# Loads of v and z moved to SyncE's queue with casts on the engines, later places for work that waits for transfers, and one more block of scores turned

## The chip, the cores and the metric

The kernel runs on one core of one Trainium2 chip. The metric is the time of one execution in microseconds (us) on the device; several runs are taken and their median stands for the kernel. The core has a matrix engine (TensorE, PE in the profile, with PEld for its weight loads), VectorE (DVE), ScalarE (ACT), GpSimd (POOL) and SyncE (SP), which here only issues transfers. Each engine works through its own list of instructions in order and waits on semaphores for the others. Transfers are issued from an engine's queue and run on 16 DMA engines.

## The reference

Two stages follow each other, for 8 batches of 3,200 rows:

```python
# stage 1: gated attention, u and v (8, 3200, 256), z (8, 3200, 64)
scores = (1 / S) * z @ z.T                 # S = 3200, symmetric
x = u * (np.maximum(scores, 0) ** 2 @ v)
# stage 2: token mixing, w_q and w_k (256, 64), w_out (256, 256)
wq, wk = x @ w_q, x @ w_k
mixed = (1 / 8) * (wq @ wk.T) @ x          # computed as wq @ (wk.T @ x)
out = np.maximum(mixed, 0) @ w_out
```

All inputs and the output are fp32. The kernel multiplies in fp16 and accumulates in fp32.

## The kernel before

**Tiles and stages.** A batch's 3,200 rows are 25 tiles of 128, in seven groups: six of 512 columns (four tiles) and a last one of 128. For a group `gi` and a row tile `ti`, `scores` (L263) multiplies a tile of z by the group's columns. Two such tiles make a pair, in one PSUM slot of 128 x 1,024; there are two slots, shared with the other small products. `first_stage` (L286 on ScalarE, L290 on VectorE) evicts the pair through a relu into `g`, `second_stage` (L306 on ScalarE, L308 on GpSimd) squares it into `at` in fp16 (16 buffers). `second_product` (L351) multiplies `at` by v into accumulators, in two halves of a group; `gate` (L368, L369, L388) sums the two accumulators of a half and multiplies by u into `x_sb`.

**Turned blocks.** The scores are symmetric, so the block of groups (gi, gj) is also the transpose of the block (gj, gi). `is_turned` says which blocks are computed once and transposed by a DMA (`turn` in `second_stage`, L330, into `tt` or `ttl`): those with `gj` at most two groups behind `gi` (`FAR = 2`), and all that end in the last group. `SKIP` takes one out in batch 0; `EXTRA`, empty before, adds blocks in the other batches. The others are computed twice.

**Stage two.** `turn_x` (L400) transposes x by a DMA, `projections` (L417) makes queries and keys, `turn_keys` (L436) transposes the keys, `double` (L448) doubles them, `heads` (L455) sums keys times x, `mix` (L483) and `proj` (L521) make the output, which `proj_out` (L546, L551) scales and SyncE stores (L552).

**Loads.** In batch 0, z and v come in pieces (L110, L113). For the next batches `load_v` (L150, five pieces of five tiles) and `load_z` (L156, one piece) are issued from GpSimd's queue, and the transfer itself changes fp32 to fp16. `turn_z` (L163) transposes z by four DMAs on SyncE's queue. u is loaded on SyncE's queue (L174).

**The order.** Nothing schedules at run time. While the program is built, a planner in the kernel keeps a clock for each engine (`clock`, `give`), takes one step of TensorE after another, and so writes out the order of every engine's instructions. Its main loop takes a waiting extra step (keys, heads, mix, proj), a pair (`use_pair`) or an accumulation step (`acc_step`); pairs run ahead of the accumulation by `lead` steps. Transfers of SyncE wait in `moves` with a ready time and a due time; `flush` sends the one that is due first once the planned queue is free, and `send` adds the planned time of issue (`issue`) and of the DMA engines (`takes`), with a backlog of `RING`, and says when it lands (`LANDS` later). What needs a transfer is given a place after that time: x after `XWAIT`, a turned block's rows 0.5 us after landing, keys at landing. `squares` chooses ScalarE or GpSimd with `SPARE`, `choose` ScalarE or VectorE with `BIAS`.

Of the kernel before, what the change touches and what calls it, by code (L numbers as in the profile page):

```python
# [16 lines left out]
def kernel(  # L17
# [48 lines left out]
    pg = ctx.enter_context(tc.tile_pool(name="pg", bufs=7))  # L66
# [80 lines left out]
    def load_v(b, n0, nn):  # L147
        if n0 == 0:
            vs[b] = pv.tile([P, NT, D], FP16, tag="v_sb", name="v_sb")
        nc.gpsimd.dma_start(out=vs[b][:, n0 : n0 + nn, :], in_=rows(v, b)[:, n0 : n0 + nn, :])  # L150
# [3 lines left out]

    def load_z(b):
        nc.gpsimd.dma_start(out=zn[:, 1 : NT + 1, :], in_=rows(z, b))  # L156
# [54 lines left out]
    EXTRA = []  # L211
# [388 lines left out]
    MIXES = 10.0  # L600
# [9 lines left out]
    RING = 2.0  # L610
# [47 lines left out]
    UNTIL = 24.0  # L658
# [36 lines left out]
    def squares():  # L695
        while pending and pending[0][0] <= clock[PE] + 0.3:
# [9 lines left out]
            for (b, gi, gj, _, nn, _, _), turn in second_stage(p, g, ways):  # L706
# [4 lines left out]
                    done + SLACK, due + SLACK, 1.28, 0.21 * n, turn,  # L711
# [20 lines left out]
    def use_keys(b, gi):  # L732
# [17 lines left out]
        if not final:  # L750
            move(
                done + SLACK, done + 10.0, 1.28, 0.21 * n, lambda: turn_keys(b, gi),
                lambda t: at_time(t, lambda: double(b, gi)),
# [63 lines left out]
    def project_out(b, gi, ps, ready):  # L817
# [14 lines left out]
        move(done + SLACK, done + 6.0, 0.55, 1.6, stores[0], landed)  # L832

    def push(takes):
        give(POOL, clock[PE], 0.6)
        dma_at[0] = max(dma_at[0], clock[PE]) + takes

    Z0 = 24
    ZWAIT, ZDUE, ZSTEP, ZSTEP0 = 14.0, 32.0, 7.0, 5.0
    V0 = 56  # L840
    V1 = 10

    def batch_begun(b, t):
        if b + 1 < B:
            t0 = max(t + 6, Z0)
            at_time(t0, lambda: (load_z(b + 1), push(3.0)))
            step = ZSTEP if b else ZSTEP0
            for i, (_, m0, m1) in enumerate(ZTURNS):
                move(
                    t0 + ZWAIT + step * i, t0 + ZDUE + step * i, 1.28, 0.21 * (m1 - m0),  # L850
                    lambda i=i: turn_z(b + 1, i),
                    lambda t, i=i: z_ready.update({(b + 1, i): t}),
                )
            for i in range(5):
                at = t + 20 + 13 * i if b else V0 + V1 * i
                at_time(at, lambda i=i: v_loaded(b + 1, 5 * i, 5))

    def v_loaded(b, n0, nn):
        load_v(b, n0, nn)
        push(2.5)  # L860
        for n in range(n0, n0 + nn):
            v_at[b, n] = dma_at[0] + 5.0
# [7 lines left out]
    def group_begun(b, gi, t):  # L870
        if gi == 0:
            batch_begun(b, t)
        if gi + 1 < NG:
            move(max(t + 2, clock[POOL] + SLACK), t + 7, 0.55, 1.6, lambda: load_u(b, gi + 1))
        elif b + 1 < B:
            move(max(t + 2, clock[POOL] + SLACK), t + 7, 0.55, 1.6, lambda: load_u(b + 1, 0))

    SPARE = 0.5
    BIAS = 0.2
    XDUE = 5.0  # L880
    XWAIT = 2.0
    LATE = 0.5

    def half_done(b, gi, half):
# [10 lines left out]
        if half == halves(gi)[-1]:  # L895
            n = 8 if widths[gi] == W else 2
            move(
                t + SLACK, t + XDUE, 1.28, 0.21 * n, lambda: turn_x(b, gi),
# [122 lines left out]
    move(10.0, 14.0, 0.55, 1.6, lambda: load_u(0, 0))  # L1021
# [5 lines left out]
    lead = 140  # L1027
    turn_about = False
    while groups or work or current["left"]:
# [10 lines left out]
                and (x[1] != "proj" or all(t + 2.0 <= now for t in stored[-2:]))  # L1040
# [134 lines left out]
```

## Time and profile before

| | us |
|---|---|
| median of 3 runs | 775.03 |
| lowest, highest | 774.68, 778.61 |
| the profiled execution | 773.15 |
| its span, first to last instruction | 770.9 |
| mean granted TensorE clock | 0.997 |

The page of the profile shows each engine's busy time as a share of the span, 28,221 instructions in all. A group's line names the kernel's line, the engine, the operation, what it writes and reads, the count, then busy time and mean of one in nanoseconds, and the idle time of the engine just before with what ended it. The windows give busy time per engine in a stretch of the span. The chain of waits follows the work that ended last back from the last instruction. For transfers, a view gives the time from issue to landing. Busy TensorE time is modelled from pipelined products; two products of 64 rows each run side by side, so their durations overlap.

### The profile page before, as it was taken

How to read it: one execution, taken by the hardware profiler on the slowest of the kernel's cores; microseconds unless marked ns; L12 is line 12 of the kernel's file. 1: busy time of each engine (PE TensorE's matmuls, PEld its weight loads, DVE VectorE, ACT ScalarE, POOL GpSimd, SP SyncE). 2: the span in 40 equal slices, each digit the busy share in tenths (PEclk: the TensorE clock that was granted, in tenths of full speed). 3: DMA queues.
4: the chain of work that ended last, by engine and by line, in shares of the span. 5: the costliest groups of instructions: out<-in, count | busy, mean ns of one | idle time of the engine just before them, and what ended most of it. 6: DMA issues, size and time to landing. Idle time of an engine off the chain costs nothing.

```text
span 770.9 us, 28221 instructions
## 1 busy us (share of the span) xinstructions
PE 761.7 (99%) x12408; PEld 678.4 (88%) x12408; DVE 510.5 (66%) x537; ACT 561.2 (73%) x647; POOL 591.1 (77%) x496
## 2 busy tenths in 40 slices
PE   8999999999999999999999999999999999999996
PEld 7889998888898888989889988998889989898884
DVE  6775876675787566765677756765667476675645
ACT  7785876778758678875788677877777676777734
POOL 8796788789687778666778687887878887888740
PEclk9999999999999999999999999999999999999998
DMA  8999999999999999999899999999999998979625
GB/s 199 130 187 182 167 204 173 160 212 194 194 162 189 194 209 190 182 213 203 153 190 162 188 231 163 219 145 160 262 156 192 184 190 211 201 143 203 152 84 191
DMA packets 307114, 141.09 MB, mean 183 GB/s; under 512 B 285744, under 2 KB 288432, under 8 KB 306992
## 3 DMA queue, kind: packets, MB, share of 16 engines
q1 hardware_dynamic: 300224, 123.13, 85.0%
q0 software_dynamic: 6624, 15.98, 14.8%
q8 instruction: 97, 1.59, 0.9%
q14 instruction: 25, 0.20, 0.1%
q10 hardware_dynamic: 144, 0.20, 0.1%
HBM read 59.64 MB, written 26.21 MB: 111 GB/s over the span
## 4 chain that ended last, share of the span: by engine, by line
PE 94%; POOL 2%; DVE 1%; DMA 1%; ACT 1%; issue 1%; POOLq 0%; SPq 0%; DVEq 0%; ACTq 0%
PE acc L351 68%; PE sc L263 13%; PE fo L521 6%; PE qk L417 3%; PE qk L455 2%; POOL at L308 2%; PE mx L483 1%; DMA z<-in_z_dram 1%; POOL x_sb L388 1%; DVE g L290 0%; ACT g L286 0%; DVE fo L546 0%; DMA xT_sb<-x_sb 0%; PE hd L455 0%; ACT at L306 0%
## 5 line engine op out<-in xcount | busy, mean ns | idle before, releaser
L351 PE MATMUL acc<-v_sb,at 64*128 64x256 f16 x7344 | 504.7, 269 | 0.0
L308 POOL TENSOR_TENSOR at<-g 128x1024 f16<-128x1024 f32 (+1 forms) x218 | 402.3, 1859 | 71.6 <-ACT g L286 29.1
L351 PEld LDWEIGHTS <-at 64*128 64x128 f16 x7344 | 407.2, 94 | 48.1 <-issue 4.8
L290 DVE TENSOR_SCALAR g<-sc 128x1024 f32<-128x1024 f32 (+2 forms) x285 | 338.5, 1203 | 122.8 <-PE sc L263 114.3
L306 ACT ACTIVATE at<-g 128x1024 f16<-128x1024 f32 (+2 forms) x255 | 257.2, 1023 | 21.8 <-DVE g L290 17.8
L286 ACT ACTIVATE g<-sc 128x1024 f32<-128x1024 f32 (+2 forms) x186 | 183.2, 989 | 76.8 <-PE sc L263 75.0
L388 POOL TENSOR_TENSOR x_sb<-both,u_sb 128x512 f16<-128x512 f32 (+1 forms) x112 | 135.8, 1217 | 81.6 <-DVE both L369 77.7
L263 PE MATMUL sc<-zT 64*128 64x512 f16 x924 | 188.1, 375 | 1.4 <-DVE g L290 0.6
L351 PE MATMUL acc<-v_sb,tt 64*128 64x256 f16 x2272 | 163.4, 269 | 0.0
L351 PEld LDWEIGHTS <-tt 64*128 64x128 f16 x2272 | 126.2, 94 | 10.3
L369 DVE TENSOR_TENSOR both<-acc,both 128x512 f32<-128x512 f32 (+1 forms) x104 | 69.6, 670 | 21.4 <-ACT both L368 17.0
L263 PEld LDWEIGHTS <-zT 64*128 64x128 f16 x924 | 61.2, 94 | 7.6 <-issue 3.9
L368 ACT COPY both<-acc 128x512 f32<-128x512 f32 (+1 forms) x69 | 39.0, 565 | 38.7 <-PE acc L351 36.1
L546 DVE TENSOR_SCALAR fo<-fo 128x1024 f32<-128x1024 f32 (+1 forms) x28 | 32.4, 1166 | 46.6 <-PE fo L521 46.6
L509 ACT ACTIVATE rt<-mx 128x1024 f16<-128x1024 f32 x39 | 39.9, 1024 | 12.6 <-PE mx L483 12.1
L521 PE MATMUL fo<-wo,rt 128*128 128x256 f16 x386 | 46.6, 273 | 0.5 <-ACT rt L505 0.5
L521 PEld LDWEIGHTS <-rt 128*128 128x128 f16 x386 | 36.2, 98 | 8.4 <-issue 3.6
L431 ACT CAST qk<-qk 128x512 f16<-128x512 f32 (+1 forms) x47 | 25.3, 539 | 24.6 <-PE qk L455 20.0
L368 DVE COPY both<-acc 128x512 f32<-128x512 f32 (+1 forms) x35 | 23.6, 674 | 21.2 <-PE acc L351 19.9
L470 DVE TENSOR_TENSOR ha<-qk,ha 128x512 f32<-128x512 f32 x37 | 25.5, 689 | 14.4 <-ACT qk L431 14.1
L551 ACT ACTIVATE fo<-fo 128x1024 f32<-128x1024 f32 (+2 forms) x23 | 22.5, 978 | 16.5 <-PE fo L521 15.8
L417 PE MATMUL qk<-xT_sb,wqk 64*128 64x256 f16 (+1 forms) x404 | 32.3, 265 | 0.0
(55 smaller groups left out, 282.9 us busy)
## 6 DMA issues: line engine op xcount, KB each, us to landing
u_sb<-in_u_dram SPq DMA_DIRECT2D x48, 512.0 KB, 4.8
out_dram<-fo SPq DMA_DIRECT2D x46, 512.0 KB, 5.1
v_sb<-in_v_dram POOLq DMA_DIRECT2D x35, 320.0 KB, 6.0
zn<-in_z_dram POOLq DMA_DIRECT2D x7, 400.0 KB, 7.8
tt<-at SPq DMA_TRANSPOSE x143, 4.7
u_sb<-in_u_dram SPq DMA_DIRECT2D x8, 128.0 KB, 2.9
out_dram<-fo SPq DMA_DIRECT2D x4, 256.0 KB, 3.3
xT_sb<-x_sb SPq DMA_TRANSPOSE x56, 5.4
```

Of the source, the lines that this page charges most:

```text
L263: nc.tensor.matmul(out=sc[h][:, 0:gw] if banks else sc[:, h, 0:gw], lhsT=z_cols(b, h, ti * P, P), rhs=z_cols(b, h, gs, gw), start=True, st ...
L286: nc.scalar.activation(out=g[:, hs, 0:w], in_=part, func=RELU, scale=GSCALE)
L290: nc.vector.tensor_scalar(out=g[:, hs, 0:w], in0=part, scalar1=0.0, scalar2=GSCALE, op0=AOP.max, op1=AOP.mult,)
L306: nc.scalar.square(out=out, in_=g[:, hs, 0:w])
L308: nc.gpsimd.tensor_mul(out=out, in0=g[:, hs, 0:w], in1=g[:, hs, 0:w])
L351: nc.tensor.matmul(out=accs[half, r][:, ds((j % 2) * D, D)], lhsT=weights(b, gi, ti, j)[top(r), :], rhs=vs[b][top(r), ti, :], start=(first ...
L368: copy(out=both[:, 0 : n * D], in_=accs[half, 0][:, 0 : n * D])
L369: nc.vector.tensor_add(out=both[:, 0 : n * D], in0=accs[half, 1][:, 0 : n * D], in1=both[:, 0 : n * D])
L388: nc.gpsimd.tensor_mul(out=xs[b, gi][:, 0:n, :, r, :].rearrange("p n c d -> p (n c) d"), in0=both[:, 0 : n * D].rearrange("p (m d) -> p m ...
L417: nc.tensor.matmul(out=ps[:, r, 0 : n * P], lhsT=wqk[top(r), c, :, :].rearrange("p t h -> p (t h)"), rhs=xTs[b, gi][top(r), 0:n, c, :], st ...
L509: nc.scalar.activation(out=out, in_=part, func=RELU)
L521: nc.tensor.matmul(out=banks[r][:, ds(j * D, D)], lhsT=flat[:, ds((dc * n + j) * P, P)], rhs=wo[:, dc, :], start=(dc == 0 and j == 0), sto ...
```

## The change

v and z of the next batch are loaded by SyncE's queue as fp32, in ten parts (`PARTS`: one of z, nine of v) and then cast to fp16 by ScalarE or GpSimd (`cast_part`). Most parts land in a piece of the next batch's v tile that has not been filled yet, the others in two staging tiles (`pst`); a part that uses a place again is sent once the casts that empty it are planned to be done. For room, the `g` tiles go from 7 buffers to 6. z is sent from 6 us after a batch's beginning, and the planner places a part's cast 6 us after its planned landing.

`EXTRA` gets the block of groups 0 and 3, so in batches 1 to 7 it is computed once and turned.

The planner's figures change: more time between a landing and what needs it (`XWAIT` 2 to 9, keys 4, turned rows 3.5, stores 4 against 2), other costs of a transfer, a backlog of 1.5, `MIXES` 10 to 8, `lead` 140 to 180, `SPARE` 0.5 to 0.1, `BIAS` 0.2 to −0.2, `UNTIL` 24 to 16. `UNTIL` is the time up to which a pair's squares may be split between two engines.

```diff
-    pg = ctx.enter_context(tc.tile_pool(name="pg", bufs=7))
+    pst = ctx.enter_context(tc.tile_pool(name="pst", bufs=1))
+    pg = ctx.enter_context(tc.tile_pool(name="pg", bufs=6))
...
-    def load_v(b, n0, nn):
-        if n0 == 0:
+    STAGES = (3, 2)
+    PARTS = [
+        (False, 0, 25, 12.5, 0),
+        (True, 0, 3, 6, 0),
+        (True, 3, 5, 15, 1),
+        (True, 8, 2, 11, 2),
+        (True, 10, 3, None, 0),
+        (True, 13, 2, None, 0),
+        (True, 15, 2, 21, 3),
+        (True, 17, 3, None, 5),
+        (True, 20, 2, None, 6),
+        (True, 22, 3, None, 8),
+    ]
+    stage_of = {}
+
+    def load_part(b, i):
+        is_v, n0, nn, slot, _ = PARTS[i]
+        if i == 0:
             vs[b] = pv.tile([P, NT, D], FP16, tag="v_sb", name="v_sb")
-        nc.gpsimd.dma_start(out=vs[b][:, n0 : n0 + nn, :], in_=rows(v, b)[:, n0 : n0 + nn, :])
+        size, what = (D, v) if is_v else (dqk, z)
+        if slot is None:
+            k = STAGES.index(nn)
+            stage = pst.tile([P, nn * D], FP32, tag=f"st{k}", name="st")[:]
+        else:
+            at = int(slot * D)
+            stage = vs[b][:].rearrange("p n d -> p (n d)")[:, at : at + 2 * nn * size].bitcast(FP32)
+        stage_of[b, i] = stage.rearrange("p (n d) -> p n d", d=size)
+        nc.sync.dma_start(out=stage_of[b, i], in_=rows(what, b)[:, n0 : n0 + nn, :])
+
+    def cast_part(b, i, m0, m1, by_act):
+        is_v, n0, _, _, _ = PARTS[i]
+        copy = nc.scalar.copy if by_act else nc.gpsimd.tensor_copy
+        out = vs[b][:, n0 + m0 : n0 + m1, :] if is_v else zn[:, 1 + m0 : 1 + m1, :]
+        copy(out=out, in_=stage_of[b, i][:, m0:m1, :])
...
-    def load_z(b):
-        nc.gpsimd.dma_start(out=zn[:, 1 : NT + 1, :], in_=rows(z, b))
...
-    EXTRA = []
+    EXTRA = [(0, 3)]
...
-    MIXES = 10.0
+    MIXES = 8.0
...
-    RING = 2.0
+    RING = 1.5
...
-        dma_at[0] = max(dma_at[0], begun) + takes
         sp_at[0] = max(begun + issue, dma_at[0] - RING)
+        dma_at[0] = max(dma_at[0], begun + max(issue, 0.9)) + takes
         if landed:
-            landed(max(sp_at[0], dma_at[0]) + LANDS)
+            landed(dma_at[0] + LANDS)
...
-    UNTIL = 24.0
+    UNTIL = 16.0
...
-                row_at[b, gj, starts[gi] // P + n] = t + 0.5
+                row_at[b, gj, starts[gi] // P + n] = t + TURNS
...
-                lambda t: at_time(t, lambda: double(b, gi)),
+                lambda t: at_time(t + KEYS, lambda: double(b, gi)),
...
+    Z1 = 6
+    VTIMES = [0, 4, 18, 23, 28, 34, 40, 46, 53, 60]
+    V0 = 0.75
+    CASTS = 6.0
+    KEYS = 4.0
+    TURNS = 3.5
+    STORES = 4.0
...
     def batch_begun(b, t):
...
+        if b == 0:
+            nc.gpsimd.memset(zn[:, 0 : NT + 2 : NT + 1, :], 0.0)
+        t0 = max(t + Z1, Z0)
+        sent[b + 1], cast[b + 1] = 0, [0, 0.0]
+        for i, (is_v, _, nn, _, after) in enumerate(PARTS):
+            at = t0 + VTIMES[i] * (1.0 if b else V0)
+            move(
+                at, at + 8.0, 0.45, 0.2 + 1.5 * nn * (D if is_v else dqk) / 1024,
+                lambda i=i: part_sent(b + 1, i),
+                lambda t, i=i: at_time(t + CASTS, lambda: part_landed(b + 1, i)),
+                lambda i=i, after=after: sent[b + 1] == i and cast[b + 1][0] >= after
+                and (not after or cast[b + 1][1] + SLACK <= clock[PE]),
+            )
...
+    def part_landed(b, i):
...
+        size, most = (D, 3) if is_v else (dqk, 9)
+        for m0 in range(0, nn, most):
+            m1 = min(nn, m0 + most)
+            n = (m1 - m0) * size
+            a, c = (max(clock[x], clock[PE]) for x in (ACT, POOL))
+            t_act, t_pool = 0.19 + 0.00084 * n, 0.15 + 0.0009 * n
+            by_act = a + SPARE < c and (a + t_act <= shut() + LATE or a + 2.5 < c)
+            cast_part(b, i, m0, m1, by_act)
...
-    SPARE = 0.5
-    BIAS = 0.2
+    SPARE = 0.1
+    BIAS = -0.2
     XDUE = 5.0
-    XWAIT = 2.0
+    XWAIT = 9.0
...
-    lead = 140
+    lead = 180
...
-                and (x[1] != "proj" or all(t + 2.0 <= now for t in stored[-2:]))
+                and (x[1] != "proj" or all(t + STORES <= now for t in stored[-2:]))
```

More of the change, by code (lines that the diff above doesn't have):

```diff
@@ L830, in landed @@
                 stored[i] = t
[L832 to L836, printed above, removed]
+        move(done + SLACK, done + 6.0, 0.45, 1.7, stores[0], landed)
     Z0 = 24
-    ZWAIT, ZDUE, ZSTEP, ZSTEP0 = 14.0, 32.0, 7.0, 5.0
-    V0 = 56
-    V1 = 10
-    def batch_begun(b, t):
[L844 to L848, printed above, removed]
+    Z1 = 6
@@ L873, in group_begun @@
         if gi + 1 < NG:
-            move(max(t + 2, clock[POOL] + SLACK), t + 7, 0.55, 1.6, lambda: load_u(b, gi + 1))
+            move(max(t + 2, clock[POOL] + SLACK), t + 7, 0.45, 1.7, lambda: load_u(b, gi + 1))
         elif b + 1 < B:
-            move(max(t + 2, clock[POOL] + SLACK), t + 7, 0.55, 1.6, lambda: load_u(b + 1, 0))
-    SPARE = 0.5
-    BIAS = 0.2
+            move(max(t + 2, clock[POOL] + SLACK), t + 7, 0.45, 1.7, lambda: load_u(b + 1, 0))
+    SPARE = 0.1
+    BIAS = -0.2
     XDUE = 5.0
-    XWAIT = 2.0
+    XWAIT = 9.0
     LATE = 0.5
```

38 lines of the change are left out of this document (23 added, 15 removed).

## The prediction

> **What bounds the kernel now.** I read the page's engine line first, then TensorE's waits, the windows, the chain of waits and the groups by form. The page opens with:
>
> ```profile
> PE 761.7 (99%) x12408; PEld 678.4 (88%) x12408; DVE 510.5 (66%) x537; ACT 561.2 (73%) x647; POOL 591.1 (77%) x496
> q1 hardware_dynamic: 300224, 123.13, 85.0%
> q0 software_dynamic: 6624, 15.98, 14.8%
> ```
>
> All that TensorE waited for, longest first:
>
> ```profile
> PE warm L144 <- DVE wo L996: 1.0, 1, 1.0
> PE sc L263 <- DVE g L290: 0.6, 2, 0.4
> PE fo L521 <- ACT rt L505: 0.5, 1, 0.5
> PE ztp L130 <- POOL zd L124: 0.4, 1, 0.4
> PE sc L263 <- ACT g L286: 0.3, 1, 0.3
> PE qq L417 <- DMA xT_sb<-x_sb: 0.2, 1, 0.2
> ```
>
> The windows (PE, weight load, DVE, ACT, POOL busy; clock; DMA share; GB/s):
>
> ```profile
> 0.00:20.00 20.00, 18.05 (x232) 14.52 (x234) 13.46 (x17) 14.29 (x18) 16.59 (x21) 1.00 0.80 194
> 20.00:40.00 20.00, 19.84 (x331) 17.73 (x329) 14.71 (x16) 14.57 (x18) 15.61 (x11) 1.00 0.95 142
> 40.00:60.00 20.00, 19.42 (x314) 16.90 (x310) 15.29 (x15) 16.62 (x18) 18.85 (x18) 1.00 1.19 178
> 100.00:720.00 620.00, 619.89 (x10221) 555.17 (x10219) 412.54 (x427) 462.52 (x525) 492.66 (x406) 1.00 1.04 188
> 720.00:771.00 51.00, 44.54 (x642) 35.83 (x637) 26.59 (x34) 24.34 (x39) 18.85 (x17) 0.96 0.47 146
> ```
>
> From 100 to 720 us TensorE is busy for 619.89 of 620 us at the full clock, while the other three stand idle for 127 to 207 us. So between the ends only a change in TensorE's work can gain, and others can only lose, by making it wait. What it waited for a transfer in the whole run is 0.2 us. The idle time sits at the ends: 20.00 − 18.05, 0.16 and 0.58 us in the first 60 us (2.7 together), and the last 20 us.
>
> **The change, part by part.** *Fewer score pairs.* One block of 4 x 4 tiles per batch is turned instead of computed a second time, in seven batches: 4 tiles each, 28 score products, 14 pairs. In the changed order of instructions TensorE has 888 score products of 512 columns in place of 916; the products into the accumulators stay 10,000 (7,120 + 2,496 + 384; 224 of them read a turned block instead of a computed one). The price of a pair, from the chain and from two pieces of the timeline:
>
> ```profile
> by line: PE acc L351 68.3%; PE sc L263 12.7%; PE fo L521 5.8%; PE qk L417 2.8%; PE qk L455 2.4%; POOL at L308 1.6%; PE mx L483 1.4%; DMA z<-in_z_dram 0.6%; POOL x_sb L388 0.5%; issue 0.5%; DVE g L290 0.5%; ACT g L286 0.4%; DVE fo L546 0.3%;
> 30.46 4.37 PE acc L351 x80
> 734.85 0.38 PE L263 MATMUL sc<-zT 64*128 64x512 f16 x2
> ```
>
> 12.7% of 770.9 us over the 462 pairs of before is 0.212 us; 80 products of 256 columns in 4.37 us are 0.109 per two, so 0.219 for two of 512. At most a pair is its whole 0.38 us, the tail included in which the next products already run. 14 pairs: 3.0 us (0.212), up to 5.3 (0.38). I take 3.0: the chain counts what nothing overlaps, and the second way agrees.
>
> *Evictions and squares.* Each pair less frees about 1.0 or 1.2 us on ScalarE or VectorE and 1.06 or 1.9 on ScalarE or GpSimd. *Casts.* v and z now land as fp32 and are cast by engines: per batch five parts of 768 and five of 512 columns of v and 1,600 columns of z in three, over seven batches 91 casts, 64 on ScalarE and 27 on GpSimd. Durations:
>
> ```profile
> L290 DVE TENSOR_SCALAR g<-sc 128x1024 f32<-128x1024 f32 x278 | 335.2, 1221 | 121.8 <-PE sc L263 113.3 <-POOL at L308 3.3 <-ACT g L286 1.8
> L286 ACT ACTIVATE g<-sc 128x1024 f32<-128x1024 f32 x175 | 178.8, 1023 | 75.0 <-PE sc L263 73.2 <-POOL kx L448 0.9 <-POOL hs L477 0.6
> L306 ACT ACTIVATE at<-g 128x1024 f16<-128x1024 f32 x240 | 250.8, 1056 | 21.8 <-DVE g L290 17.8
> L308 POOL TENSOR_TENSOR at<-g 128x1024 f16<-128x1024 f32 x211 | 396.5, 1893 | 70.0 <-ACT g L286 29.1 <-DVE g L290 29.0 <-issue 9.6
> L124 ACT CAST zd<-z 128x512 f16<-128x512 f32 x1 | 0.6, 619 | 1.8 <-DMA z<-in_z_dram 1.8
> L124 ACT CAST zd<-z 128x256 f16<-128x256 f32 x1 | 0.4, 404 | 1.2 <-DMA z<-in_z_dram 1.2
> L124 POOL CAST zd<-z 128x512 f16<-128x512 f32 x1 | 0.6, 609 | 0.9 <-DMA z<-in_z_dram 0.9
> L124 POOL CAST zd<-z 128x384 f16<-128x384 f32 x1 | 0.5, 503 | 1.4 <-DMA z<-in_z_dram 1.4
> L150 POOL DMA_DIRECT2D v_sb<-in_v_dram x35 | 20.7, 591 | 0.0
> ```
>
> By the slopes (0.84 and 0.83 ns a column) 768 columns take 0.83 and 0.82 us. ScalarE: 25 x 0.62 + 27 x 0.83 + 12 of z, some 46 us; GpSimd: 10 x 0.61 + 8 x 0.82 + 9 of z, some 18. GpSimd is rid of 42 issues at 0.591 us (25 us, not in its busy time). With the evictions that move between the engines in the new order I get ScalarE about 606 us (79%), GpSimd 625 (81%), VectorE 465 (60%). All stay under TensorE, so on average the casts cost nothing. Their cover is the distance by which score pairs run ahead: counting TensorE's work in the order, half of the pairs stood at least 8.3 us ahead of their first use before and stand 12.5 ahead after (the larger lead of 180 steps against 140); the shortest beyond the first 20 us was 3.8 and is 4.9. A cast of 0.83 us, or one that waits 3 us for its data, is inside that; a wait of 5 us at the shortest place isn't, and all that is queued behind the cast on ScalarE (an eviction of scores, for which TensorE's slot waits) is late by the rest.
>
> The tightest stage is 20 to 60 us: 95.6 of 120 us are busy on the three engines. By 55 us of TensorE's work the new order has 1.5 pairs more and nine casts more (about 4 + 6 us), so the reserve shrinks from 24 to 14 us. I take nothing for it; between −1 and +2 us.
>
> *Loads on SyncE's queue, and the turns.*
>
> ```profile
> L330 SPq DMA_TRANSPOSE tt<-at x143: 1231/1354/5576, 17.1 to 713.4; - x143
> L174 SPq DMA_DIRECT2D u_sb<-in_u_dram x56: 327/529/1814, 5.0 to 738.3; - x56
> u_sb<-in_u_dram SPq DMA_DIRECT2D x48, 512.0 KB, 4.8
> u_sb<-in_u_dram SPq DMA_DIRECT2D x8, 128.0 KB, 2.9
> v_sb<-in_v_dram POOLq DMA_DIRECT2D x35, 320.0 KB, 6.0
> ```
>
> SyncE issues 77 loads more (70 of v, 7 of z) and 14 turns more: 77 x 0.53 + 14 x 1.35 = 60 us on a queue that takes its instructions in order. Past them go the turns of blocks, x, keys and z and the stores. What a late turn meets: by the order, a turned block is first used 28 us of TensorE's work or more after its last scores (26 before, leaving out the first two blocks), transposed x 20 us or more outside the last batch, transposed z 14 us or more (25 in all but the first). The last part of v is cast 4 to 10 us ahead of its batch's first product, in the first of these batches 1.3 us behind it; that part holds the last three of 25 tiles. The later places (x 9 us after its landing against 2, keys 4, turned blocks 3.5, stores 4) give each transfer 2 to 7 us more room and add no product. A load that lands 3 us late is covered; I take 0, with 0 to 7 us open (one us per batch).
>
> *One buffer fewer for the score evictions* (6 against 7), and zn's zeroing on GpSimd: VectorE waited 3.3 us for squares in all of before, behind TensorE's cover; 0.
>
> *The end.* One output projection now stands behind the last accumulation: 16 products. What they cost, from the chain, and the chain and products behind the last accumulation of before:
>
> ```profile
> 145.23 1.85 PE fo L521 x16
> 747.81 1.74 POOL x_sb L388
> 749.57 1.77 POOL x_sb L388
> 751.34 1.47 issue
> 754.52 2.34 DMA xT_sb<-x_sb
> 756.10 0.61 PE L483 MATMUL mx<-qk,hs 64*128 64x256 f16 x8 [0.17 <-DVE hs L1126]
> 756.90 0.39 PE L417 MATMUL qq<-xT_sb,wqk 64*128 64x128 f16 x4 [0.19 <-DMA xT_sb<-x_sb]
> ```
>
> The last accumulation now ends 1.85 us earlier. Behind it, the transfer landed at 756.86 us (754.52 + 2.34), when mx had been running for 0.76 us; with 1.85 us of other products ahead of it, mx takes over as the late one. What was gained ahead is given back: 0, at best −0.2.
>
> **Sum.** −3.0 us. The profiled execution took 773.15 us (770.9 and 2.25 around the span), 1.9 under the median of the three runs shown; its 770.1 corresponds to 775.03 − 3.0 = 772.0 us. About 0.5%, 3.9 us, is what a measurement of this kernel can tell from no change: under 771.15 is faster, over 778.9 slower.
>
> **The rivals.**
>
> *More than the pairs goes.* If the earlier lead also removes the waits of the first 60 us (2.7 us idle there, 1.0 of it the wait for the first memset), or a pair is worth nearer 0.38 us, the gain is 4 to 5.3 us: 769.7 to 771.0, say 770.5. For it: the limit is TensorE, and the waits on score evictions all lie in the stages that the new constants touch. Against: that stage gets more work, not less. Chance 0.32.
>
> How long v's loads of before took to land, all 35 of them:
>
> ```profile
> DMA to landing us min/median/max: 4.5/6.0/9.0
> ```
>
> *The one queue falls behind (slower).* v and z had a queue of their own; now 77 loads and all turns follow one another. For it: the two queues' packet times add up to 99.8% of the span, and the DMA share is 1.04; if none of that is slack, 14 turns of 256 KB more (3.67 MB at 85.0% of 770.9 us for 123.13 MB, 5.3 us a MB) cost 19.5 us, 791. Against: those times overlap, and TensorE waited 0.2 us for transfers. It decides once the last parts of v land later than their 4 to 10 us of cover: then each of seven batches begins late, at 1 to 3 us each (9.0 us at most against 6.0 in the middle is the spread of v's landings) 7 to 21 us, less 3.0: 779 to 793, say 782. The Trainium skill, DMA: Bandwidth & Descriptors, section SWDGE vs HWDGE vs iDMA, says that the two kinds feed different queues inside a DMA engine, which serves them in turn; by it a turn used to share with a load and now stands behind it. No row here shows the second case. By the rows of u, 384 KB more land 1.9 us later, so a turn behind the 800 KB of z would land some 4 us later, inside its 28. Chance 0.14.
>
> *The pairs go and the time stays.* The 3.0 us come back as short waits of TensorE on evictions between 20 and 60 us and at the batch starts: 774 to 775.5. It needs the 14 us of reserve to lie in the wrong places. Chance 0.06.
>
> **How the numbers follow.** The forecast as it stands has 0.48: 772.0, its own range 770.8 to 774. With the third case, "within 0.5%" has 0.54, faster 0.32, slower 0.14. From 769.5, the bottom of the first rival, to 779.0, where the slower case begins, leaves out about 0.04 below and 0.13 above.
>
> **What would show it.** After: 888 products of 512 columns on the score line, TensorE still over 99% busy from 100 to 720 us, its last accumulation some 5 us earlier (3.0 and 1.85), ScalarE and GpSimd near 79 and 81%, casts of 0.8 us with hardly any idle time before them, and no wait of TensorE for a transfer over 1 us. Wrong would be: TensorE's idle time in the middle in whole microseconds at the seven batch starts, ended by a cast or a DMA (the slower case); or a first window as full as the others (the faster one).

## The result and the profile after

The changed kernel takes 783.8 us (median of 6 runs, 782.69 to 789.5) against 775.06 for the kernel before in the same call (6 runs, 774.53 to 778.61): 1.0115 times, 95% interval 1.008 to 1.0149. It is slower by some 9 us, where 772.0 was forecast. The ratios here and below leave out runs over 1.5% longer than the fastest of their kernel, which in e1 are seven of ten, so that its median and its ratio tell different things. The profiled execution took 783.7 us, its span is 781.9.

The page of the changed kernel opens so (engines, queues, chain by engine; the chain of before by engine stands behind it for comparison):

```profile
PE 761.8 (97%) x12380; PEld 676.5 (87%) x12380; DVE 468.8 (60%) x505; ACT 593.9 (76%) x702; POOL 599.3 (77%) x495
q1 hardware_dynamic: 325088, 155.47, 99.7%
q0 software_dynamic: 576, 1.64, 1.1%
PE 83%; DMA 7%; ACT 3%; POOL 2%; issue 2%; SPq 1%; DVE 1%; ACTq 0%; DVEq 0%; POOLq 0%
```

```profile
PE 94%; POOL 2%; DVE 1%; DMA 1%; ACT 1%; issue 1%; POOLq 0%; SPq 0%; DVEq 0%; ACTq 0%
```

TensorE has 28 products fewer (12,380 against 12,408), and no other engine came near TensorE's load. But the chain now runs through transfers for 7% of the span instead of 1%, and the packets of q1 alone fill 99.7% of the 16 DMA engines' span. The windows say where TensorE stands idle (columns as in the prediction):

```profile
0.00:20.00 20.00, 16.86 (x208) 12.93 (x209) 11.85 (x15) 14.49 (x19) 15.45 (x22) 1.00 0.74 183
20.00:40.00 20.00, 19.70 (x325) 17.52 (x323) 14.40 (x14) 16.31 (x19) 18.17 (x11) 1.00 0.92 188
40.00:60.00 20.00, 20.00 (x340) 19.19 (x337) 15.20 (x15) 17.53 (x21) 18.52 (x16) 1.00 0.95 211
100.00:720.00 620.00, 611.37 (x10048) 543.52 (x10043) 371.31 (x398) 483.26 (x562) 487.32 (x395) 1.00 1.08 210
140.00:180.00 40.00, 38.49 (x611) 34.64 (x607) 24.23 (x26) 29.99 (x37) 26.37 (x23) 1.00 1.12 202
340.00:380.00 40.00, 36.39 (x556) 31.31 (x553) 19.18 (x22) 27.48 (x35) 23.53 (x21) 0.96 1.16 226
420.00:460.00 40.00, 38.58 (x639) 34.01 (x635) 23.31 (x25) 30.69 (x37) 31.09 (x26) 1.00 1.03 196
720.00:782.00 62.00, 53.85 (x797) 44.55 (x792) 29.96 (x38) 28.54 (x43) 23.25 (x23) 0.97 0.51 154
```

The idle time of TensorE grows from 9.2 us (770.9 − 761.7) to 20.1 (781.9 − 761.8). From 100 to 720 us it is 8.63 us, where it was 0.11; in the first 60 us 3.44 against 2.69; in the last window 8.05 (the span ends at 781.9) against 6.36 (it ended at 770.9). That is the span's loss of 11.0 us but for 0.1: busy time rose by 0.1 although, by the forecast's price, 3.0 us of work went. Some 1.5 us of that is the clock of 0.96 in the 36.39 busy us of 340 to 380; where the rest went no view shows.

What TensorE waited for, and then what the other engines waited for from a transfer:

```profile
PE sc L291 <- ACT g L314: 5.0, 6, 3.4
PE ztp L131 <- POOL zd L125: 1.2, 1, 1.2
PE mx L511 <- ACT rt L537: 1.1, 1, 1.1
PE qk L445 <- ACT rtl L537: 1.0, 1, 1.0
PE sc L291 <- ACT fo L579: 0.9, 1, 0.9
```

```profile
POOL kx L476 <- DMA kx<-qk: 19.2, 7, 4.5
ACT v_sb L181 <- DMA st<-in_v_dram: 7.6, 6, 1.8
ACT v_sb L181 <- DMA v_sb<-in_v_dram: 5.4, 2, 3.8
POOL v_sb L181 <- DMA v_sb<-in_v_dram: 3.9, 1, 3.9
ACT fo L579 <- DMA out_dram<-fo: 2.2, 2, 1.2
```

TensorE still waits for no transfer. It waits for ScalarE, above all for score evictions; and ScalarE and GpSimd now wait for transfers, 38.3 us in these rows. In the kernel before, beside the first loads of z, the rows of that kind hold 4.3 us:

```profile
POOL kx L448 <- DMA kx<-qk: 2.2, 2, 2.0
POOL x_sb L388 <- DMA xT_sb<-x_sb: 1.3, 1, 1.3
ACT fo L551 <- DMA u_sb<-in_u_dram: 0.8, 1, 0.8
```

The longest stop shows how one passes to the other. SyncE's queue from 344 us on, then the chain, ScalarE and TensorE (timelines: start, duration, instruction, idle time before it and what ended it):

```profile
344.81 2.61 SPq L358 DMA_TRANSPOSE tt<-at  x2
347.46 2.38 SPq L191 DMA_TRANSPOSE zT<-zn  x1
349.94 0.53 SPq L202 DMA_DIRECT2D u_sb<-in_u_dram  x1
350.52 1.23 SPq L428 DMA_TRANSPOSE xT_sb<-x_sb  x1
351.81 0.57 SPq L175 DMA_DIRECT2D v_sb<-in_v_dram  x1
```

```profile
351.81 4.34 DMA v_sb<-in_v_dram
```

```profile
356.17 0.62 ACT L181 CAST v_sb<-v_sb 128x512 f16<-128x512 f32 x1 [3.79 <-DMA v_sb<-in_v_dram]
356.69 1.02 ACT L314 ACTIVATE g<-sc 128x1024 f32<-128x1024 f32 x1
```

```profile
353.56 0.82 PE L379 MATMUL acc<-v_sb,at 64*128 64x256 f16 x11
357.76 0.41 PE L291 MATMUL sc<-zT 64*128 64x512 f16 x2 [3.38 <-ACT g L314]
```

SyncE has three turns (two of scores, one of z), a load of u and a turn of x without a gap ahead of a part of v. The part is issued at 351.81 and lands in 4.34 us, which is not long. But ScalarE has come to its cast and waits 3.79 us; behind the cast stands the eviction of a pair of scores; and TensorE, in order too, stops for 3.38 us at the next pair, which needs the slot that this eviction frees. The same pattern (a part of v, its cast, an eviction or a copy, TensorE) ends idle times of TensorE near 157 and 460 us (0.93 and 0.48 us); at 343.8 us GpSimd had waited 3.98 us for keys, and TensorE 0.22 us behind it.

### The profile page after: what moved, and what is told of

It reads as the page before. It is cut to its first block, busy times and chain, and to the rows that moved or that the text cites. A ratio compares the mean times of both kernels' runs of the same rounds, so it can differ in the third digit from the quotient of the medians.

```text
span 781.9 us, 28324 instructions
## 1 busy us (share of the span) xinstructions
PE 761.8 (97%) x12380; PEld 676.5 (87%) x12380; DVE 468.8 (60%) x505; ACT 593.9 (76%) x702; POOL 599.3 (77%) x495
## 3 DMA queue, kind: packets, MB, share of 16 engines
q1 hardware_dynamic: 325088, 155.47, 99.7%
## 4 chain that ended last, share of the span: by engine, by line
PE 83%; DMA 7%; ACT 3%; POOL 2%; issue 2%; SPq 1%; DVE 1%; ACTq 0%; DVEq 0%; POOLq 0%
PE acc L379 60%; PE sc L291 12%; PE fo L549 4%; DMA st<-in_v_dram 3%; PE qk L445 2%; PE qk L483 2%; DMA out_dram<-fo 2%; POOL at L336 1%; DMA v_sb<-in_v_dram 1%; PE mx L511 1%; ACT g L314 1%; DMA z<-in_z_dram 1%; ACT at L334 1%; DVE g L318 1%; ACT fo L579 1%
## 5 line engine op out<-in xcount | busy, mean ns | idle before, releaser
L379 PE MATMUL acc<-v_sb,at 64*128 64x256 f16 x7120 | 486.1, 270 | 0.5 <-POOL at L336 0.3
L336 POOL TENSOR_TENSOR at<-g 128x1024 f16<-128x1024 f32 (+2 forms) x231 | 417.7, 1821 | 80.6 <-DVE g L318 71.5
L379 PEld LDWEIGHTS <-at 64*128 64x128 f16 x7120 | 392.7, 94 | 49.0 <-issue 4.7
L318 DVE TENSOR_SCALAR g<-sc 128x1024 f32<-128x1024 f32 (+2 forms) x249 | 297.0, 1202 | 170.0 <-PE sc L291 153.8
L314 ACT ACTIVATE g<-sc 128x1024 f32<-128x1024 f32 (+2 forms) x208 | 204.8, 992 | 59.7 <-PE sc L291 56.9
L334 ACT ACTIVATE at<-g 128x1024 f16<-128x1024 f32 (+2 forms) x228 | 231.3, 1039 | 8.2 <-DVE g L318 6.2
L379 PEld LDWEIGHTS <-tt 64*128 64x128 f16 x2496 | 145.0, 94 | 10.1 <-issue 0.2
L579 ACT ACTIVATE fo<-fo 128x1024 f32<-128x1024 f32 (+2 forms) x43 | 40.9, 996 | 20.3 <-PE fo L549 18.1
L476 POOL COPY kx<-kx 128x128 f16<-128x128 f16 (+1 forms) x99 | 25.6, 288 | 19.2 <-DMA kx<-qk 19.2
L539 DVE TENSOR_SCALAR rt<-mx 128x1024 f16<-128x1024 f32 x17 | 20.8, 1225 | 26.6 <-PE mx L511 26.6
```

The source lines that it names most:

```text
L314: nc.scalar.activation(out=g[:, hs, 0:w], in_=part, func=RELU, scale=GSCALE)
L318: nc.vector.tensor_scalar(out=g[:, hs, 0:w], in0=part, scalar1=0.0, scalar2=GSCALE, op0=AOP.max, op1=AOP.mult,)
L334: nc.scalar.square(out=out, in_=g[:, hs, 0:w])
L336: nc.gpsimd.tensor_mul(out=out, in0=g[:, hs, 0:w], in1=g[:, hs, 0:w])
L379: nc.tensor.matmul(out=accs[half, r][:, ds((j % 2) * D, D)], lhsT=weights(b, gi, ti, j)[top(r), :], rhs=vs[b][top(r), ti, :], start=(first ...
L579: nc.scalar.mul(out=flat_out[:, sl], in_=part, mul=FINAL_SCALE)
```

## The experiments

The table has all of them, with the kernel before of the same call.

| run | what it is | us, median (range) | before, same call | ratio (95%) |
|---|---|---|---|---|
| e1_no_loads | after, v and z loaded as before | 785.8 (773.29–800.94) | 775.99 | 1.0019 (0.997–1.0068) |
| e2_no_block | after without the block | 780.32 (776.53–782.53) | 775.99 | 1.0042 (1.0014–1.0071) |
| e3_gpsimd_queue | after, the fp32 loads from GpSimd's queue | 790.7 (784.12–798.09) | 775.99 | 1.0165 (1.0081–1.0248) |
| e4_casts12 | after, casts placed 6 us later | 807.75 (806.48–811.15) | 775.99 | 1.0416 (1.0376–1.0455) |
| e5_places_only | before with the new figures only | 777.95 (776.42–779.67) | 773.99 | 1.0056 (1.0035–1.0076) |
| e6_before_new_costs | before with the new transfer costs only | 788.32 (785.05–797.99) | 773.99 | 1.0175 (1.0148–1.0202) |
| e7_old_costs | after with the old transfer costs | 780.86 (779.77–782.55) | 773.99 | 1.0094 (1.0076–1.0113) |
| e8_block_costs15 | before, the block, a turn at 0.2 + 0.15 n | 780.26 (774.31–783.76) | 773.99 | 1.01 (1.0073–1.0127) |
| e9_light_stores | after, stores cut to a quarter | 773.7 (770.71–778.67) | 775.93 | 0.9968 (0.9942–0.9995) |
| e10_light_stores_new_costs | e6 with the same cut | 789.36 (787.19–800.53) | 775.93 | 1.0169 (1.0139–1.0198) |
| e11_block_only | before and the block, nothing else | 792.11 (790.64–797.88) | 775.93 | 1.0219 (1.0172–1.0266) |
| e12_block_mid | e8 with half the new distances | 775.02 (773.54–782.26) | 775.93 | 1.0 (0.9975–1.0026) |
| e13_before_light_stores | before with the cut of e9 | 773.96 (772.02–780.35) | 775.77 | 0.9994 (0.9965–1.0023) |
| e14_turn_cost15 | after, a turn at 0.2 + 0.15 n | 776.72 (773.13–785.18) | 775.77 | 1.0015 (0.9981–1.0048) |
| e15_turn_cost16 | after, 0.2 + 0.16 n | 783.53 (775.55–785.16) | 775.0 | 1.0082 (1.005–1.0115) |
| e16_turn_cost17 | after, 0.2 + 0.17 n | 782.32 (777.69–790.51) | 775.0 | 1.0081 (1.0047–1.0114) |

One more reading is used below. The planner writes an order, and for each transfer a time at which it is to be issued. Set against the trace, with TensorE's own drift from the plan at that moment taken off, that tells how far SyncE trails the plan. It is worked out from all of SyncE's transfers and the starts of all accumulation products of each profiled execution; the column after it is the sum of the durations of those transfers on SyncE's queue:

| run | SyncE behind its plan, us: median / 90% / most | SyncE issuing, us | last accumulation planned / run |
|---|---|---|---|
| before | −1.4 / 1.1 / 4.1 | 612 | 756.2 / 751.4 |
| after | 3.9 / 10.1 / 14.2 | 667 | 749.3 / 759.1 |
| e2_no_block | 0.5 / 6.9 / 13.6 | 627 | 755.0 / 758.4 |
| e5_places_only | 2.0 / 8.1 / 12.9 | 628 | 753.1 / 757.0 |
| e7_old_costs | −0.6 / 4.1 / 6.3 | 654 | 765.4 / 759.2 |
| e9_light_stores | 1.9 / 9.8 / 15.5 | 645 | 749.3 / 757.2 |
| e14_turn_cost15 | 5.6 / 9.6 / 12.2 | 670 | 750.4 / 753.5 |
| e16_turn_cost17 | 1.6 / 3.9 / 5.7 | 671 | 763.6 / 754.5 |

The kernel before has an order in which SyncE is ahead of its plan and TensorE beats it by 5 us. The changed kernel's order is shorter by 7 us on paper, and TensorE comes out 10 us behind it. How far SyncE trails does not rank the times, though: e14 trails as far as the changed kernel and is level with before, e16 trails far less and is 0.8% slower.

**Which part costs: e1, e2, e5, e11.** e1 takes away the loads and keeps the rest:

```diff
-        nc.sync.dma_start(out=stage_of[b, i], in_=rows(what, b)[:, n0 : n0 + nn, :])
+        nc.gpsimd.dma_start(out=vs[b][:, n0 : n0 + nn, :], in_=rows(v, b)[:, n0 : n0 + nn, :])
(and load_z, the seven g buffers and the load times of before)
```

> The block and the later places stay; v and z are loaded as before, by GpSimd's queue with the cast in the transfer. Theory A (transfers on SyncE's queue come late, casts and key copies wait for them in order on ScalarE and GpSimd, and TensorE waits for the evictions behind them): 771 to 773 us, the 3.0 us of the 14 pairs, and waits of ScalarE and GpSimd for transfers as small as before (under 5 us together). Theory B (the casts' own work fills ScalarE and GpSimd): the same 771 to 773 us. Theory C (the turned block, or the order that the new places make): 780 to 785 us.

It scattered over 28 us, too much for its time to decide anything. Its profile, of a run of 785.5 us where the ratio rests on three of 773 to 784, is only an indication: without a cast of the next batches' v and z, or a load of them on SyncE's queue, the waits for transfers were there all the same.

```profile
POOL kx L448 <- DMA kx<-qk: 24.3, 10, 5.9
ACT at L306 <- DMA ttl<-at: 9.3, 1, 9.3
PE sc L263 <- ACT g L286: 7.0, 1, 7.0
```

e2 is one line of the changed kernel:

```diff
-    EXTRA = [(0, 3)]
+    EXTRA = []
```

> Loads on SyncE's queue and later places stay; the block of groups 0 and 3 is computed twice again. Theory A: 3.0 us more of TensorE's work, 14 turns fewer on the queue, and so fewer late transfers, but not none: 776 to 784 us. Theory B: 14 pairs more to evict and square on engines that are full: 786 us or more. Theory C, if it is the block: 773 to 776 us.

e5 has all the new figures of the planner (places, costs of transfers, `lead`, `SPARE`, `BIAS`, `UNTIL`, `MIXES`) in the kernel before, no casts and no block:

```diff
-    RING = 2.0
+    RING = 1.5
-                    done + SLACK, due + SLACK, 1.28, 0.21 * n, turn,
+                    done + SLACK, due + SLACK, 1.25, 0.2 + 0.13 * n, turn,
-    XWAIT = 2.0
+    XWAIT = 9.0
-    lead = 140
+    lead = 180
(and the other figures of the diff)
```

> The kernel before with all the planner's new figures, but v and z loaded by GpSimd's queue and no further block turned. Theory D (the planner now counts a turn of a full block at 1.24 us where SyncE's queue, in its long unbroken rows, takes 1.8 to 2.1 us of it, so the written order asks for transfers faster than they come): SyncE trails TensorE here too, but with 14 turns and 77 loads fewer it catches up between; 774 to 779 us. If the loads or the block alone are to blame: 774.5 to 776 us, no difference from before.

Figures alone: 1.0056. Figures and loads: 1.0042. So without the block the 77 loads on SyncE's queue and the 91 casts cost nothing that these runs can tell, about 0.3% either way. With the block it is 1.0115: the block, which takes 3 us of products away by the forecast's price, makes the kernel some 0.7% (5 to 6 us) slower. e11 adds the block to the kernel before:

```diff
-    EXTRA = []
+    EXTRA = [(0, 3)]
```

> The kernel before with the block of groups 0 and 3 turned and nothing else: old costs, old places, loads by GpSimd. If turning a block is worth its 14 pairs wherever it is put: 771 to 773 us. Theory D: at the old costs 14 turns of 1.7 us more do not fit between the others, the planner itself puts products later, and TensorE waits in the written order for late turns' places: 775 to 790 us, with SyncE on time.

It is the slowest of the block's versions but e4, at 1.0219. Here the planner, which counts a full turn at 1.68 us, sees the lack of transfer time itself and stretches the order: the last accumulation is planned at 777 us against 756. So the block cannot be had under the old count, and the change's lower count is what lets the order be written short.

**The queue: e3.** The order of all engines stays, the fp32 loads go out from GpSimd's queue:

```diff
-        nc.sync.dma_start(out=stage_of[b, i], in_=rows(what, b)[:, n0 : n0 + nn, :])
+        nc.gpsimd.dma_start(out=stage_of[b, i], in_=rows(what, b)[:, n0 : n0 + nn, :])
```

> The changed kernel with one word changed: the fp32 loads of v and z go out by GpSimd's queue, the casts stay where they are. Theory A: 77 issues leave SyncE's queue, which catches up: 773 to 777 us, with GpSimd's 0.6 us an issue beside it. Theory B: the casts are all there: 783 us or a little more. Theory C: 783 us.

1.0165, no better than on SyncE's queue. But its profile loses the time in another way: in one large stop early on, at a turn of z that stands behind a turn of scores which held SyncE for 7.57 us, and hardly any later:

```profile
80.00:120.00 40.00, 28.78 (x469) 27.36 (x465) 18.49 (x21) 21.21 (x27) 28.23 (x25) 0.87 0.98 157
100.00:720.00 620.00, 618.65 (x10230) 548.88 (x10227) 378.57 (x405) 490.56 (x572) 530.35 (x466) 1.00 1.11 213
```

```profile
PE sc L291 <- DMA zT<-zn: 11.2, 1, 11.2
```

From 100 to 720 us TensorE is idle for 1.35 us here, where it was 8.63 in the changed kernel. So e3 doesn't clear the loads on SyncE's queue of the stops in mid-run; it shows that the other queue brings no gain in time. Why that turn took 7.57 us is open; three loads of v had been issued from GpSimd's queue from 73.97 us on, and the row of turns began at 74.28.

Taking the loads from SyncE's queue doesn't take the transfers from the DMA engines. That agrees with the Trainium skill, DMA: Bandwidth & Descriptors, section Issuing engines are not separate DMA queues: transfers of all engines run on the same 16 DMA engines, and another issuing engine saves only the time of the issue.

**More room for the casts: e4.**

```diff
-    CASTS = 6.0
+    CASTS = 12.0
```

> The changed kernel with each cast placed 12 us after its planned landing in place of 6. Theory A: the waits of ScalarE and GpSimd for v and z go, those for keys stay: 774 to 779 us. Theory B and theory C: 782 to 785 us, since the work and the turns are the same.

1.0416, a miss. What hangs on a cast (the turns of z, then the scores of the next batch, and v) is pushed back with it, so the planned last accumulation moves from 749 to 782 us. It tests no wait, since the order itself got longer.

**The count of a transfer: e6, e7, e8, e12.** e6 gives the kernel before the new transfer costs (as in e5's first two pairs of lines, with those of u, z, x, keys and stores) and nothing else; e7 gives the changed kernel the old ones.

> The kernel before with the planner's new costs of a transfer alone (a turn 1.25 us of the queue and 0.2 + 0.13 us a 128-column block of the DMA engines, backlog 1.5, landing counted from the DMA engines), and the old narrow places behind them. Theory D: SyncE loses the lead that it had over the plan, and the narrow places let TensorE wait: 776 to 785 us. Otherwise: 775 to 776 us.

> The changed kernel, loads, block and later places and all, with the planner's old costs of a transfer (1.28 us, 0.21 us a block, backlog 2.0). Theory D: the waits of ScalarE and GpSimd for transfers shrink to the size of before (under 10 us together, 41 in the changed kernel), while the order itself holds TensorE back where the counted transfers no longer fit: 773 to 785 us, with the idle time ended by score evictions and not behind casts. Theory A (the loads on the one queue, however they are planned): waits for transfers as in the changed kernel, 782 to 786 us.

The new costs without the later places lose 1.75%: the order expects landings earlier than they come, and TensorE waits for x itself (`PE qk` for a transfer, 6.6 us) and GpSimd 31.5 us for keys (sums of their rows in the waits). So the lower count needs the later places. With the old costs in the changed kernel, SyncE is on time again (−0.6) and the waits for keys are gone, but the order is 16 us longer on paper (765.4 against 749.3) and the time is 1.0094: paying in the order or paying in waits comes to nearly the same. e8 and e12 give the block to the kernel before with a count between (in e8 the old places, in e12 `XWAIT` 5, keys 2, turned rows 2):

```diff
-    EXTRA = []
+    EXTRA = [(0, 3)]
-                    done + SLACK, due + SLACK, 1.28, 0.21 * n, turn,
+                    done + SLACK, due + SLACK, 1.25, 0.2 + 0.15 * n, turn,
(in both the other new costs of e6; e12 also:)
-    XWAIT = 2.0
+    XWAIT = 5
-                row_at[b, gj, starts[gi] // P + n] = t + 0.5
+                row_at[b, gj, starts[gi] // P + n] = t + 2
-                lambda t: at_time(t, lambda: double(b, gi)),
+                lambda t: at_time(t + 2, lambda: double(b, gi)),
```

> The kernel before with the block of groups 0 and 3 turned, and a turn counted between the old and the new cost (0.2 + 0.15 us a block, 1.4 us for a full one); loads by GpSimd, places, lead and the rest as before. Theory D: the queue is ahead or at most a few us behind: 771 to 775 us, a gain of up to the 3 us of the 14 pairs. If the 14 turns are themselves too much for the DMA engines: 778 us or more.

> The block turned on the kernel before, a full turn counted at 1.4 us (as in the run of 780 us with the old places), with places between the old and the new ones: x 5 us after landing, keys 2, turned rows 2. Theory D: the same queue, but 2 to 3 us more room for each transfer: 771 to 777 us, and less spread from run to run. If the 14 turns overrun the DMA engines whatever the places: 779 us or more.

Between e8 and e12 only the places differ, and they are worth 1%: 1.01 against 1.0, with intervals that don't meet. e12 is, with e14, the best version with the block that computes everything: level with before. The 3 us of saved products don't come through in any of them.

**Is it the transfers' supply? e9, e10, e13.** The order of the changed kernel stays as it is, every instruction in its place; each store takes one tile of its four. The packets of q1 carry 136.86 MB in place of 155.47.

```diff
-                out=rows(out, b)[:, n0 + at : n0 + at + n, :],
-                in_=flat_out[:, sl].rearrange("p (n d) -> p n d", d=D),
+                out=rows(out, b)[:, n0 + at : n0 + at + 1, :],
+                in_=flat_out[:, sl].rearrange("p (n d) -> p n d", d=D)[:, 0:1, :],
```

> The changed kernel, its written order untouched, with each store of the output cut to its first tile of 128 rows (left out: three quarters of the output of the full groups), so that some 17 MB fewer run on SyncE's queue in the same number of issues. If the DMA engines are what the written order overruns (theory D): SyncE catches up, the waits of casts and key copies for transfers halve at least, and 773 to 778 us. If it is the order itself, or the casts' work: 782 to 785 us.

> The kernel before with the same cut of the stores as in e9: each store takes only the first of its four tiles, so three quarters of the output are left out. Control to e9. If the transfers are what the changed order overruns, the kernel before, whose matrix engine waited 0.2 us for transfers, gains little: ratio 0.996 to 1.000 (772 to 776 us), and the recovery of e9 (1.0115 to 0.9968) belongs to the change. If lighter stores simply make any of these kernels faster, it gains like e9, some 11 us: 763 to 766.

The changed kernel goes from 1.0115 to 0.9968, that is 11 us (0.0147 of 775); the kernel before from 1 to 0.9994, nothing that can be told. So in this order the loss goes with the bytes that the DMA engines have to move. With lighter stores the change is ahead of before by 0.3%, in the size of the 3.0 us of products, but its interval overlaps that of e13.

By which path the bytes cost the time is less clear. The profile that was taken of e9 is of its slowest run (778.67). In it the casts and key copies still wait 29.2 us for transfers, against 36.6 in the changed kernel, so these waits did not halve as expected, and SyncE still trails by 9.8 us at 90%. Which waits are gone in the faster runs is not shown by a trace. Some of the gain lies at the end: from the end of the last accumulation to the end of the span the profiled execution takes 22.6 us in the changed kernel and 19.3 in e9, 19.2 in the kernel before and 17.4 in e13. e10 makes the same cut in e6:

> The kernel before with the new costs of a transfer alone (788 us), order untouched, and the stores cut in the same way (left out: three quarters of the output of the full groups). Theory D: 774 to 780 us. If that order is slow by itself: 786 to 790 us.

No recovery (1.0169 against 1.0175), against the expectation. There the places are narrow, and TensorE waits for x directly:

```profile
PE qk L417 <- DMA xT_sb<-x_sb: 15.9, 4, 7.3
```

So the bytes of the transfers cost the changed kernel its time; they are not what e6 suffers from.

**Is the count the lever? e14, e15, e16.** The changed kernel with a turn of n tiles counted higher, in its four places:

```diff
-                    done + SLACK, due + SLACK, 1.25, 0.2 + 0.13 * n, turn,
+                    done + SLACK, due + SLACK, 1.25, 0.2 + 0.15 * n, turn,
(0.16 in e15, 0.17 in e16)
```

> The changed kernel with one figure between the old and the new: a turn of n tiles counted as 0.2 + 0.15 n in place of 0.2 + 0.13 n (a full block 1.40 us against 1.24; the old count was 1.68; rows of turns in the trace take 1.84 to 2.06 each). If the too low count is what makes the written order outrun the transfers, SyncE trails less and the casts wait less, at a somewhat longer order: 776 to 781, below the 783.8 of the changed kernel. If the count doesn't matter, 782 to 786.

> The changed kernel with the turn of n tiles counted as 0.2 + 0.16 n (a full block 1.48 us). One step further on the way of e14 (0.15 n: 1.0015 of before) towards the old count of 1.68 (e7: 1.0094, where the order itself had got longer). If the best place lies between, SyncE trails less than in e14 and the order is only a little longer: ratio 0.997 to 1.004, 773 to 779. If already 0.15 n was at the edge of a longer order: 1.004 to 1.009.

> The changed kernel with the turn of n tiles counted as 0.2 + 0.17 n (a full block 1.56 us). By the same reading the order's own length now grows faster than the waits shrink: ratio 1.000 to 1.008, 775 to 782. At or below e15 the count should have gone further still.

e14 comes out at 1.0015 as expected, but not for the expected reason: SyncE trails its plan as much as in the changed kernel (5.6 us in the middle, 9.6 at 90%), and the waits for transfers are hardly smaller.

```profile
POOL kx L476 <- DMA kx<-qk: 17.9, 10, 3.7
ACT v_sb L181 <- DMA st<-in_v_dram: 5.5, 4, 2.6
PE sc L291 <- ACT g L314: 0.9, 3, 0.3
```

What is gone is the last step: TensorE's wait for evictions, 5.0 us in the changed kernel and 0.9 here, though TensorE now waits 3.3 us for x itself. It fits late transfers that meet casts and copies with no needed eviction behind them; that this is luck of the order is a reading, not a test. One step further the time is back at 1.008 (e15, the worse of its two expected cases), and e16, whose order is 14 us longer on paper, has the same. So the count is no smooth lever: each figure shifts the whole order, and between e14 and e15 that is worth 0.7%.

**What is settled and what is not.** The loss goes with the bytes of the transfers (e9 against e13), and the block and the planner's figures bring it (e2, e5). Without the block the loads and casts bring none (e2 against e5); with it they are not cleared, since e1 scattered and e3 loses its time elsewhere. Which of e5's figures costs its 0.6% is not separated. That late transfers stop TensorE through an engine that works in order and the two score slots is seen in the trace of the changed kernel at several places; that this path carries the whole loss is not shown. A kernel with more slots, or with casts on an engine that evicts no scores, was not tried. No version here that computes everything is faster than the kernel before by more than can be told.

## Why the prediction was wrong

*Fewer score pairs, −3.0 us.* Right in kind: 888 products of 512 columns stand on the score line, as forecast (row below), and with lighter stores the change is ahead by 0.3%, hardly clear of e13. With the real stores all of it is eaten.

```profile
L291 PE MATMUL sc<-zT 64*128 64x512 f16 x888 | 191.0, 378 | 6.3 <-ACT g L314 5.0 <-ACT fo L579 0.9 <-DVE g L318 0.3
L181 ACT CAST v_sb<-st 128x768 f16<-128x768 f32 x17 | 14.1, 829 | 1.8 <-DMA st<-in_v_dram 1.7
L181 POOL CAST v_sb<-st 128x768 f16<-128x768 f32 x4 | 3.3, 826 | 0.2 <-DMA st<-in_v_dram 0.2
```

*Casts.* Their duration was forecast at 0.83 and 0.82 us and measured at 0.829 and 0.826; ScalarE at 606 us (593.9 measured), GpSimd 625 (599.3), VectorE 465 (468.8). The sizes held. The cover did not: it was taken from the distance between a pair and its first use, 12.5 us in the middle. What stops TensorE is not that use but the next pair of scores, which needs a free slot, and of those there are two. The prediction named this ("an eviction of scores, for which TensorE's slot waits") and then priced it by the larger cover: it asked for a wait of 5 us, and a wait of 3.79 us cost 3.38.

*Loads on SyncE's queue and the turns.* Of the 60 us more of issue time 55 came: 612 became 667. "A load that lands 3 us late is covered; I take 0" held without the block (e2 against e5) and not with it: in the longest stop ScalarE waits 3.79 us for a load and TensorE loses 3.38. The term asked what each transfer's user could bear, not whether the queue could follow the plan at all. A full turned block holds SyncE for 1.85 us in the mean of its 157 (1.89 in the mean of the 143 of before, which the trace would have told); the old plan counted 1.68, the new one 1.25. Over 157 turns the difference of 0.6 us is 94 us of queue time that the plan doesn't know of, some of it in gaps. The landing times stayed as they were (turned blocks 4.7 us in the middle before and after, keys 4.0); the transfers were issued late.

*The step that failed* is this term of 0 and the ground given for it, the part of the change that was read as free: "The later places … give each transfer 2 to 7 us more room and add no product." The same hunks lower what the planner counts for a turn, from 1.68 us to 1.25, and that was not costed. A place is worth its distance from the real landing; the new ones were laid from planned issue times that SyncE misses by 3.9 us in the middle and 10.1 at 90%. In place of the 0 stands a loss of 11.8 us (783.8 − 772.0), of which lighter stores give back 11. The figures alone cost 0.6% (e5), and the block, with its 14 turns, the rest. Nor was the count the whole mistake: with the old one the order grows by 16 us on paper and the time is 1.0094 (e7). Written short or written long, the order does not get the added transfers for nothing.

*The rivals.* That more than the pairs goes (0.32) did not show: the first 60 us lost 3.44 us to idle time, not less than the 2.69 of before. Nor did the waits between 20 and 60 us that the third case (0.06) needs: TensorE is idle for 0.30 us there, where it was 0.74. The slower one had the right resource and, by luck, nearly the right time (779 to 793, say 782, against 783.8), at a chance of 0.14. Its place was wrong: it saw TensorE waiting at batch starts for the last parts of v, while the stops lie in mid-batch, at casts and key copies. Its number of 99.8% for the two queues' packets was the best single warning in the profile, and it was set aside because "TensorE waited 0.2 us for transfers". That row tells of an order built so that nothing came late, not of room for more. It also made something of the two queues becoming one. By the Trainium skill, DMA: Bandwidth & Descriptors, section SWDGE vs HWDGE vs iDMA, which the prediction named, a turn would share with a load of the other queue and now stand behind it; the median landing of turned blocks is 4.7 us before and after and 4.9 in e3, so the queues made no difference to the middle of them. The longest landing is 9.8 us before, 8.9 after and 15.6 in e3, where the loads are on the other queue.

*The end.* Forecast at 0 to −0.2; it lost 1.7 us (idle in the last window, 8.05 against 6.36). The last accumulation should have ended 5 us earlier and ended 7.6 later (about 759.3 against 751.7). Behind it the last eviction of an output waits for a store that takes 4.75 us to let go of its buffer:

```profile
770.65 4.75 DMA out_dram<-fo
```

```profile
775.50 0.60 ACT L579 ACTIVATE fo<-fo 128x512 f32<-128x512 f32 x1 [1.16 <-DMA out_dram<-fo]
```

## What to carry to other kernels

Where the queues' packet times fill the span, work on the busiest engine that is bought with more transfers need not be free, even if that engine waits for no transfer now: cut the transfers in a trial (here the stores) and see how much of the loss comes back, and cut them in the old kernel too. A change of the counts by which an order is planned is a change of the kernel and needs its own term in the sum: compare the planned issue times with the trace. Where an operation waits on an engine working in order, look for its cover in what stands behind it on that engine (here evictions that two score slots wait for), and not only in the distance to the use of its result.

## What the runs showed of the hardware

The packet times of the two queues add up to about the whole span in both kernels (99.7% and 1.1% after, 85.0% and 14.8% before), and before TensorE waited 0.2 us for them; the sum by itself doesn't say at which load transfers begin to cost time. What tells is the cut of 18.6 MB, which moves one order by 11 us and another by nothing.

Moving 77 loads from the queue that converts to one that doesn't, which raised q1's bytes by the fp32 writes (126.80 MB without the loads on it, 155.47 with), changed no time that could be told where the block was not turned (1.0042 against 1.0056).

Two long stops of TensorE came with a lower granted clock that outlasted them. In the changed kernel the stop of 3.38 us ends at 357.76 us, and the clock is 0.50 from 358 to 360 us, 0.64 from 360 to 362 and 1.00 from 362 on; over the 36.39 busy us of 340 to 380 its mean of 0.96 is an estimated 1.5 us more, on top of the 3.4. In e3 the stop of 11.2 us ends at 92.3 us, and the clock is 0.50 from 86 to 95 us and 1.00 from 96 on.

The order of a kernel's instructions is fixed, and yet its runs lie some 10 us apart: 773.07 to 782.19 in the 19 runs of the kernel before beside e1, 773.13 to 783.29 in nine of the ten of e14. A single profile shows one of several outcomes.
